# Moving loads and small stores between the stages of a backward kernel: gradient rows for a tail, zero columns of tap arrays, narrow rows

## The chip, the cores and the metric

The kernel runs on one core of one Trainium2 chip. The metric is the device time of one launch in microseconds. A profile is one execution taken by the hardware profiler; its span is a little shorter than the device time. The engines are named as in the profile: PE is TensorE (PEld its weight loads), DVE is VectorE, ACT is ScalarE, POOL is GpSimd, SP is SyncE. SP computes nothing here: it issues nearly all transfers, and SPq and ACTq in a view are the issues of SP and of ACT.

## The reference

The reference is one block of a speech model for two sequences of 4000 tokens with 144 channels, run forward and backward. It returns the output and the gradients of all eight inputs.

```python
xa = layernorm(x)
q, k, v = split(xa @ w_qkv)
glob = softmax(q @ k.T * D ** -0.5) @ v @ w_att_out          # global branch: attention
h = gelu(layernorm(x) @ w_mlp_in);  u, g = split(h)
gc = conv5(layernorm(g), dw_csgu)                            # 5 taps along the tokens
loc = (u * gc) @ w_mlp_out                                   # local branch
m = concat(glob, loc)
out = x + (m + conv5(m, dw_merge)) @ w_merge
_out, vjp = jax.vjp(forward, x, w_qkv, ..., w_merge)
return (_out, *vjp(grad_out))
```

## The kernel before

**Stages.** For each of the two sequences (index b) the kernel runs three stages: a head, attention with the local branch inside it, and a tail. A token block has 128 tokens, so a sequence has 32 blocks; a group g is four blocks, so there are 8 groups. The 144 channels don't fit 128 partitions: the first 128 go one way, and the last 16 ("narrow rows") another.

**Head** (`phase_head`). `take_go` fetches the rows of `grad_out` for one group into a tile `gs`, five shifted copies for the five taps, 720 KB, through `go_taps` (lines 1095 to 1118; group 0 takes four transfers, because the rows before the first token are zeros that POOL writes at L1106). `narrow` gathers the last 16 channels of the five copies into a tile `g80` on POOL (L1436). `stA` transposes both on PE (L1473 and L1478); ACT and DVE copy them out (L1474, L1481, the latter into `go80`). `stT` transposes the normalised input (L1486, L1490). `stB` makes Q and the gradients that enter the two branches (PE L1506 to L1515, copies on ACT L1508, L1518 and DVE L1516). In the first sequence the head also prepares weights, among them `W.c80` in `Weights.rest` (L1360, L1361). At n == 5 `spread` sends the narrow rows of the normalised input, sixteen partitions of `R`, to DRAM (L1525, tensor `R_d`) and into the arrays that attention reads (L1529).

**Attention** (`phase_attn`) runs over 32 rows of blocks and is written out by hand: `unit` makes scores and their gradients (L1975, L1979, then ACT L1987 and DVE L1989), `flip` transposes them by DMA (L1997), `yz` (L2025) and `xfill` (L2047, L2048) use them two rows later. Between these the class `Steps` places the local branch, `local_steps`, a pair of blocks at a time. A pair starts with a matmul on the wide rows and one on the narrow rows (L1803, L1804); the narrow ones lie in a tile `Rz`, 128 partitions that are zero but for the last sixteen, loaded from `R_d` (`load_R`, L1783). The convolutions of the local branch pass through four DRAM arrays (`Taps`), whose columns before the first token and after the last must be zero; the constructor writes them with two small transfers each (L1625, L1626).

**Tail** (`phase_tail`): each of its 8 groups needs a `gs` again. Groups 0, 3 and 6 take it from a pool `S.early` that exists from the start of the kernel, the others from a pool of the tail. The first tail also normalises the second sequence's input and fetches the first three `gs` tiles for its head (L2350, steps NPR - 1 to NPR + 1 of the tail, NPR = 16). At its end it copies a partial sum out (`grs`, ACT L2282) and sends it to DRAM (`gr_d`, L2283).

**What sets the order.** Every engine runs its own list in order; a wait at the head of a list holds all that is behind it. SP's list holds nearly all transfers. In the built program of before the four transfers of a tail's group 0 stand far ahead of that tail: for the first sequence among the first loads of the first head, for the second at the end of the first tail, among the loads of the second head.

Of the kernel before, what the change touches and what calls it, by code (L numbers as in the profile page):

```python
# [7 lines left out]
BF = mybir.dt.bfloat16  # L8
# [6 lines left out]
D = 144  # L15
# [1043 lines left out]
NBK = 32  # L1059
# [61 lines left out]
class Weights:  # L1121
# [3 lines left out]
    def __init__(self, k, W, tmp):  # L1125
        self.k, self.W, self.tmp = k, W, tmp
# [163 lines left out]
    def rest(self, pst, ps):  # L1290
# [67 lines left out]
        pt = ps.tile([128, 512], F32, tag="w", name="fw")  # L1358
        for v in range(2):
            nc.tensor.matmul(pt[0:80, v * DR:(v + 1) * DR], self.e5[v][0:5].rearrange("p a b -> p (a b)"), self.cw[0:5, 2 * D + 128:3 * D], start=True, stop=True)  # L1360
            nc.vector.tensor_tensor(W.c80[0:80, v, :], pt[0:80, v * DR:(v + 1) * DR], self.i80[0:80, :], op=ALU.mult)  # L1361
        for h in range(2):
            A = self.A[h]
# [75 lines left out]
def take_go(k, S, b, g, ld):  # L1439
    gs = S.gs[g] = ld.tile([128, 4, 5, D], BF, tag="gs", name="gs")  # L1440
    go_taps(k, gs, b, g, k.nc.sync)


def phase_head(k, W, b, S, nrm, ld, wts):

    nc, tc = k.nc, k.tc
    with ExitStack() as es:
# [13 lines left out]
        id_ = W.ident  # L1461
        S.QB = S.ab.tile([128, 4, 128], BF, name="QB")
        nc.vector.memset(S.QB[:], 0.0)

        def narrow(g):
            if g not in S.g80:
                narrow_go(k, S, g, ld)
# [55 lines left out]

        def spread():
            nc.sync.dma_start(S.R_d[:], R[112:128, :])  # L1525
            for q in range(2):
                for r in (2 * q, 2 * q + 1):
                    for c0, c1, x in S.XRw:
                        nc.sync.dma_start(x[32 * r:32 * r + DR, :, 0:SC], R[112:128, 0:TT_].rearrange("p (a h c) -> p a h c", h=2, c=SC)[:, c0:c1, q, :])  # L1529
# [16 lines left out]
        with tc.manual_schedule():  # L1546
            rest = None
            for g in range(3):
                if g not in S.gs:
                    take_go(k, S, b, g, ld)  # L1550
            if wts:
                wts.heads(ps_t, ps_2, lambda: nrm.stats(0))
                nrm.power(0)
                wts.taps1(0)
                wts.keys(ps_t, ps_2)
                nrm.shift(0)
                nrm.apply(0)
                narrow(0)
                wts.taps()
                wts.taps1(1)  # L1560
                nrm.stats(1)
                nrm.power(1)
                stA(0)
                take_go(k, S, b, 3, ld)
                stT(0)
                wts.rows(ps_2, 0)
                nrm.shift(1)
                nrm.apply(1)
                narrow(1)
                nrm.stats(2)  # L1570
                nrm.power(2)
                wts.rows(ps_2, 1)
                rest = wts.rest(ps_t, ps_2)
            else:
                narrow(0)
                narrow(1)
                stA(0)
                take_go(k, S, b, 3, ld)
                stT(0)
            for n in range(-1, NGR):  # L1580
                if 1 <= n + 2 < NGR:
                    stT(n + 2)
                if n == 3:
                    jit0()
                if n >= 0:
                    stB(n, *tiles())
                if 1 <= n + 2 < NGR:
                    stA(n + 2)
                if wts and n + 3 < NGR:
                    nrm.shift(n + 3)  # L1590
                    nrm.apply(n + 3)
                if n + 3 < NGR:
                    narrow(n + 3)
                if wts and n + 4 < NGR:
                    nrm.stats(n + 4)
                    nrm.power(n + 4)
                if n + 5 < NGR and n + 5 not in S.gs:
                    take_go(k, S, b, n + 5, ld)
                for f in put_dug[:len(put_dug) - n % 2]:
                    f()  # L1600
                del put_dug[:len(put_dug) - n % 2]
                if n == 5:
                    spread()
                if n == 4:
                    jit()
                if rest:
                    next(rest, None)
            for _ in rest or ():
                pass
            for f in put_dug:  # L1610
                f()
            del put_dug[:]
# [3 lines left out]
class Taps:  # L1616
# [1 line left out]

    L = 2 + NBK * 128 + 2

    def __init__(self, k, name, zero):
        self.nc = k.nc
        self.a = k.tc.dram_tile([80, self.L], BF, name=name)
        with self.nc.allow_non_contiguous_dma(reason="two columns before the first"):
            self.nc.sync.dma_start(self.a[:, 2:4], zero[0:80, 0:2])  # L1625
            self.nc.sync.dma_start(self.a[:, self.L - 4:self.L - 2], zero[0:80, 0:2])  # L1626
# [14 lines left out]
class Chan:  # L1641

    def __init__(self, k, W, pool, ps, name, zero):
        self.k, self.W, self.pool, self.ps, self.name = k, W, pool, ps, name
        self.t, self.r, self.kept, self.kept8 = {}, {}, {}, {}
        self.taps = Taps(k, name + "_d", zero)

    def put(self, p, src):  # L1650
        nc = self.k.nc
# [112 lines left out]
def local_steps(k, W, b, S, es, ps, Q):  # L1764
# [4 lines left out]
    on = es.enter_context(tc.tile_pool(name="lo_on", bufs=1, reuse_waits="tile"))  # L1769
    zero = on.tile([128, 2], BF, name="lo_zero")  # L1770
    nc.gpsimd.memset(zero[:], 0.0)
    gnC = Chan(k, W, wk, ps, "gnC%d" % b, zero)
    dgC = Chan(k, W, wk, ps, "dgC%d" % b, zero)
    S.taps = [Taps(k, n + "80_%d" % b, zero) for n in ("y", "u")]
    dws = on.tile([128, NBK // 2, 5], F32, name="dws")
    dw8 = on.tile([128, NBK // 2], F32, name="dw8")
    jg = on.tile([128, 256], BF, name="jg")
    Rz = [on.tile([128, 256], BF, name="Rz%d" % n) for n in range(2)]
    for t in Rz:
        nc.gpsimd.memset(t[:], 0.0)  # L1780

    def load_R(p):
        nc.sync.dma_start(Rz[p % 2][112:128, :], S.R_d[:, p * 256:(p + 1) * 256])  # L1783
    load_R(0)
    id_ = W.ident
    NPR = NBK // 2

    def pair(p):
# [2 lines left out]
            return tuple(((n, p - d), 0) for n, d in keys if p >= d)  # L1791
        yield 'P', 0, aft(("z", 1), ("h", 2))
        R = Rz[p % 2]
        if p + 1 < NPR:
            load_R(p + 1)
        hs = wk.tile([128, 2, 2 * D], BF, tag="hs", name="hs")
        sq = wk.tile([128, 2, 2 * D], BF, tag="sq", bufs=1, name="sq")
# [16 lines left out]
        nc.vector.tensor_tensor(a_[:], a_[:], hs[:], op=ALU.mult)  # L1814
        Q.mark("z", p)
        yield 'V', 2
        nc.scalar.activation(a_[:], a_[:], ACT.Tanh)
        yield 'V', 2, aft(("ug", 4)), .8
        h_ = wk.tile([128, 2, 2 * D], BF, tag="h_t", bufs=4, name="h_t")
# [106 lines left out]
def phase_attn(k, W, b, S):  # L1926
# [3 lines left out]
    with ExitStack() as es:  # L1930
# [137 lines left out]
        with tc.manual_schedule():  # L2068
            local_steps(k, W, b, S, es, ps_f, Q)
            for g in range(1, NGR):  # L2070
                Q.add(32 * g - 16, jit(g))
            left = list(range(NGR, 2 * NGR))
            for i in range(NBK + 2):
                if i == NBK:
                    Q.rate = Q.most = 1.8
                pr, half = i // 2 - 1, i % 2
                for c2 in range(4):
                    if 4 * i + c2 <= 4 * NBK:
                        unit(4 * i + c2)
                    for place in range(2):  # L2080
                        if place == 0 and 0 <= i - 2 < NBK:
                            yz(i - 2, c2)
                        if (i, c2, place) in ((0, 0, 0), (0, 1, 0), (0, 2, 0), (0, 3, 0), (0, 3, 1), (1, 0, 0), (1, 1, 0), (1, 1, 1)):
                            S.stB(left.pop(0), lambda: ps_y.tile([128, 2, D], F32, tag="y", name="pq"), lambda: ps_x.tile([128, 2 * D], F32, tag="x", name="pb"),
                                  lambda: xp.tile([128, 4, D], BF, tag="xs", name="dug"))
                            if not left:
                                nc.vector.memset(P[:, 2, TT_:], 0.0)
                        for f, rows in fills.get((half * 4 + c2, place), ()):
                            if 0 <= pr < NBK // 2:
                                xfill(pr, f, rows)  # L2090
                        Q.place()
                        for key, fi, h in {(0, 0): (("PT", i - 1, 1),), (1, 0): (("ST", i - 1, 1),), (2, 1): (("PT", i, 0),), (3, 1): (("ST", i, 0),)}.get((c2, place), ()):
                            if 0 <= fi < NBK:
                                flip(key, fi, h)
            while Q.tasks:
                Q.place()


def phase_tail(k, W, b, S, nrm, nxt):
# [3 lines left out]
    with ExitStack() as es:  # L2103
# [20 lines left out]
        def loads(g):  # L2124
            r = slice(g * 4, g * 4 + 4)

            one = g % 3 == 0
            gs = S.early.tile([128, 4, 5, D], BF, tag="gs", name="gs") if one else ld.tile([128, 4, 5, D], BF, tag="gs", name="gs")
            go_taps(k, gs, b, g, nc.sync)
            ug = S.early.tile([128, 4, D], BF, tag="ug", name="ug") if one else ld.tile([128, 4, D], BF, tag="ug", name="ug")  # L2130
            nc.sync.dma_start(ug[:], S.ug_d[:, r, :])
            G["ug", g], G["gs", g] = ug, gs
# [153 lines left out]
        with tc.manual_schedule():  # L2286
# [6 lines left out]
            for h in range(NPR + 5):  # L2293
# [52 lines left out]
                    dx_mm(h)  # L2346
                if hf == 0 and 0 <= g - 1 < NGR:
                    load_x(g - 1)
                if nrm and NPR - 1 <= h < NPR + 2:
                    take_go(k, nxt, 1, h - NPR + 1, nrm.ld)  # L2350
                if hf == 1 and g + 2 < NGR:
                    load_dh(g + 2)
                    loads(g + 2)
# [346 lines left out]
```

## Time and profile before

| | |
|---|---|
| device time, median of 3 runs | 1292.65 us (1290.83 to 1294.41) |
| span of the profiled execution | 1286.6 us |
| PE busy | 1210.9 us, 94% |
| DVE / ACT / POOL busy | 960.4 / 843.3 / 559.4 us |
| moved by DMA | 205.44 MB, mean 160 GB/s |

In the first sequence the head lies at 0 to 51 us, attention at 51 to 553 us and the tail from there; the second head begins at 641 us, its attention at 670 us and the last tail at 1175 us. Busy shares are means over these stages. What the edits touch is the few microseconds at the joints between stages, so the joints are read one by one.

### The profile page before, as it was taken

Reading aid. Unit: us, or ns where it says so; the run is one execution under the profiler, and the core shown is the slowest. Engines: PE = TensorE matmul, PEld = TensorE weight load, DVE = VectorE, ACT = ScalarE, POOL = GpSimd, SP = SyncE. Lnnn points to the kernel's source line nnn. Section 1 sums busy time; section 2 is a strip of 40 time slices with the busy share of each in tenths; the row PEclk is TensorE's granted clock in tenths of the full one; section 3 lists DMA queues with packets and bytes.
Section 4 is the critical chain, followed back from the end, with each engine's and each line's share of the span. In section 5 each row is a group of like instructions: output and inputs, shape, how many; then the busy total and the mean of one; then the engine's idle time right before and its main releaser. Section 6 shows DMA issues by size and latency. Waiting matters only on the chain.

```text
span 1286.6 us, 39804 instructions
## 1 busy us (share of the span) xinstructions
PE 1210.9 (94%) x15118; PEld 949.2 (74%) x15118; DVE 960.4 (75%) x3257; ACT 843.3 (66%) x2494; POOL 559.4 (43%) x1011
## 2 busy tenths in 40 slices
PE   7799999999999999989988999999999999998995
PEld 4567777777777777789964777777777777778984
DVE  7467788888788887857535677888888878885774
ACT  5677777777777766556555777776776777654542
POOL 7213444444445432356511244454544445334650
PEclk9999999999999999999988999999999999999998
DMA  7379999998898999968755798899998998998861
GB/s 232 79 144 168 144 166 157 154 160 159 157 161 150 159 166 158 161 191 220 205 168 102 142 165 149 152 164 162 160 165 150 159 166 155 162 160 179 240 165 30
DMA packets 633617, 205.44 MB, mean 160 GB/s; under 512 B 576719, under 2 KB 630948, under 8 KB 633380
## 3 DMA queue, kind: packets, MB, share of 16 engines
q1 hardware_dynamic: 626912, 197.46, 81.7%
q10 hardware_dynamic: 6500, 5.32, 1.7%
q8 instruction: 120, 1.97, 0.6%
q14 instruction: 85, 0.70, 0.2%
HBM read 46.14 MB, written 21.79 MB: 53 GB/s over the span
## 4 chain that ended last, share of the span: by engine, by line
PE 66%; DVE 14%; DMA 6%; issue 5%; ACT 4%; SPq 2%; POOL 2%; ACTq 0%; DVEq 0%; POOLq 0%
PE y L2025 15%; PE pS L1979 9%; PE X L2047 8%; PE X L2048 8%; PE pD L1979 7%; PE pS L1975 5%; DVE Sm L1989 5%; PE pc L1684 2%; PE pb L1514 2%; DMA gs<-in_grad_out_dram 2%; DVE jg L1906 2%; DMA u<-r 1%; DVE acc L2063 1%; ACT Qs L2008 1%; PE pD L1975 1%
## 5 line engine op out<-in xcount | busy, mean ns | idle before, releaser
L1989 DVE SCALAR_TENSOR_TENSOR Sm<-pD,Pm 128x500 bf16<-128x500 f32 x512 | 325.7, 673 | 92.5 <-PE pD L1979 58.6
L1987 ACT ACTIVATE Pm<-pS 128x500 bf16<-128x500 f32 x512 | 295.9, 586 | 41.4 <-PE pS L1979 38.6
L2047 PE MATMUL X<-Qs,Sm 128*128 128x144 bf16 x2048 | 285.6, 226 | 9.5 <-DVE acc L2063 9.1
L2060 POOL TENSOR_TENSOR acc<-xs,acc 128x432 f32<-128x432 f32 x150 | 169.2, 1128 | 279.8 <-ACT xs L2059 279.4
L2048 PE MATMUL X<-Bt,Pm 128*128 128x144 bf16 x2048 | 285.4, 226 | 0.6 <-DVE Bt L2012 0.6
L2048 PEld LDWEIGHTS <-Pm 128*128 128x128 bf16 x2048 | 200.2, 98 | 12.1 <-issue 11.5
L2047 PEld LDWEIGHTS <-Sm 128*128 128x128 bf16 x2048 | 200.1, 98 | 1.5 <-issue 0.9
L2025 PEld LDWEIGHTS <-PT 128*128 128x128 bf16 x2048 | 136.6, 98 | 30.7 <-issue 2.8
L2025 PEld LDWEIGHTS <-ST 128*128 128x128 bf16 x2048 | 136.4, 98 | 27.6
L2059 ACT COPY xs<-X 128x432 f32<-128x432 f32 x150 | 78.0, 520 | 111.3 <-PE X L2048 102.1
L2063 DVE TENSOR_TENSOR acc<-X,acc 128x432 f32<-128x432 f32 x180 | 104.0, 578 | 53.2 <-PE X L2048 52.7
L1987 ACT ACTIVATION_READ_ACCUMULATOR Pm<-pS 128x1 f32 x512 | 104.8, 205 | 0.0
L1975 PE MATMUL pD<-rb,QBr 16*128 16x500 bf16 x448 | 95.7, 379 | 3.5 <-DVE Sm L1989 3.0
L1979 PEld LDWEIGHTS <-BTm 128*128 128x128 bf16 x512 | 49.9, 98 | 60.0 <-issue 2.0
L1975 PE MATMUL pS<-rb,QBr 16*128 16x500 bf16 x448 | 92.1, 380 | 0.5 <-DMA rb<-Sm 0.2
L1906 DVE SCALAR_TENSOR_TENSOR jg<-gnC,dgC 128x256 bf16<-128x256 bf16 x160 | 88.9, 556 | 1.0
L1979 PEld LDWEIGHTS <-QTm 128*128 128x128 bf16 x512 | 29.0, 97 | 73.2 <-issue 73.2
L2035 POOL TENSOR_TENSOR B_t<-zd,yd 128x144 bf16<-128x144 f32 x64 | 34.0, 531 | 112.2 <-ACT zd L2034 111.8
L1979 PE MATMUL pS<-ra,QTm 128*128 128x500 bf16 x256 | 76.9, 382 | 0.0
L1979 PE MATMUL pS<-rb,QTm 128*128 128x500 bf16 x256 | 76.6, 381 | 0.0
L2025 PE MATMUL y<-ra,PT 128*128 128x144 bf16 x1024 | 74.3, 226 | 1.3 <-ACT zd L2034 1.3
L2025 PE MATMUL y<-rb,PT 128*128 128x144 bf16 x1024 | 74.3, 226 | 1.1 <-ACT zd L2034 1.1
(638 smaller groups left out, 2885.1 us busy)
## 6 DMA issues: line engine op xcount, KB each, us to landing
gs<-in_grad_out_dram SPq DMA_DIRECT2D x24, 720.0 KB
dh_d<-dh SPq DMA_DIRECT2D x32, 144.0 KB
dhr<-dh_d SPq DMA_DIRECT2D x16, 288.0 KB
gs<-in_grad_out_dram SPq DMA_DIRECT2D x8, 540.0 KB
xg<-in_x_dram SPq DMA_DIRECT2D x21, 144.0 KB
dug_d<-dug SPq DMA_DIRECT2D x16, 144.0 KB
dug<-dug_d SPq DMA_DIRECT2D x32, 72.0 KB
ug_d<-ug SPq DMA_DIRECT2D x32, 72.0 KB
```

What stands on the lines that cost most here:

```text
L1906: nc.vector.scalar_tensor_tensor(jg[:], a_[:, m:m + 256], 1.0, d_[:, 2:258], op0=ALU.mult, op1=ALU.mult, accum_out=dws[:, p, m:m + 1])
L1975: nc.tensor.matmul(o_[h][:, 0:SC], jt[i // 4][2][rr, i % 4, :], S.XR[c2][rr, 0:SC], start=True, stop=False)
L1979: nc.tensor.matmul(o_[h][:, 0:SC], jt[i // 4][w][:, i % 4, :], S.xaT[:, c0:c0 + SC], start=False, stop=True)
L1987: nc.scalar.activation(P[:, pb, c1:c1 + SC], o_[h][:, 0:SC], ACT.Exp, accum_out=ld8[:, 0, n_:n_ + 1])
L1989: nc.vector.scalar_tensor_tensor(Sm[:, pb, c1:c1 + SC], o_[h][:, 0:SC], 1.0, P[:, pb, c1:c1 + SC], op0=ALU.mult, op1=ALU.mult, accum_out=l ...
L2025: nc.tensor.matmul(y[:, w, :], src[:, jj, :], S.xaa[:, j, :], start=(j == 0), stop=(j == NBK - 1))
L2035: nc.gpsimd.tensor_tensor(S.Zn[:, i, :], zd[:], yd[:], op=ALU.add)
L2047: nc.tensor.matmul(X[:, jj, :], Sm[:, i % NP, j * 128:(j + 1) * 128], Qs[:, i % 4, :], start=(kk == 0 and jj == 0), stop=False, skip_group ...
L2048: nc.tensor.matmul(X[:, jj, :], P[:, i % NP, j * 128:(j + 1) * 128], Bt[:, i % 4, :], start=False, stop=(kk == 1), skip_group_check=True)
L2059: nc.scalar.copy(xs[:, 0:nj, :], X[:, 0:nj, :])
L2060: nc.gpsimd.tensor_tensor(a_, xs[:, 0:nj, :], a_, op=ALU.add)
L2063: nc.vector.tensor_tensor(a_, X[:, 0:nj, :], a_, op=ALU.add)
```

## The change

It moves transfers and a few instructions; the arithmetic is the same.

1. **Tail rows.** The `gs` of a tail's group 0 is fetched near the end of attention (row 32, column step 1), behind the last transposes, and no longer in a head. In the first tail the three `gs` loads for the next head start one step earlier.
2. **Zero columns.** The zero columns of the four tap arrays are sent from the first two pairs of the local steps, between other work, not all at once when the local steps are set up.
3. **Narrow rows.** The `Rz` tiles live in the head's pool and get their first two contents directly from `R` in on-chip memory, beside the other sends of `spread`; only pairs from 2 on read `R_d`.
4. **Two small orders in the first head.** The two matmuls of `c80` are issued before the two multiplications that read their bank; `narrow(0)` comes ahead of `apply(0)` on POOL.

```diff
@@ Weights.rest
         for v in range(2):
             nc.tensor.matmul(pt[0:80, v * DR:(v + 1) * DR], self.e5[v][0:5].rearrange("p a b -> p (a b)"), self.cw[0:5, 2 * D + 128:3 * D], start=True, stop=True)
+        for v in range(2):
             nc.vector.tensor_tensor(W.c80[0:80, v, :], pt[0:80, v * DR:(v + 1) * DR], self.i80[0:80, :], op=ALU.mult)
@@ phase_head
         nc.vector.memset(S.QB[:], 0.0)
+        S.Rz = [S.ab.tile([128, 256], BF, name="Rz%d" % n) for n in range(2)]
+        for t in S.Rz:
+            nc.gpsimd.memset(t[:], 0.0)
...
         def spread():
             nc.sync.dma_start(S.R_d[:], R[112:128, :])
+            for p in range(2):
+                nc.sync.dma_start(S.Rz[p][112:128, :], R[112:128, p * 256:(p + 1) * 256])
...
                 nrm.shift(0)
+                narrow(0)
                 nrm.apply(0)
-                narrow(0)
@@ Taps
-    def __init__(self, k, name, zero):
+    def __init__(self, k, name):
         self.nc = k.nc
         self.a = k.tc.dram_tile([80, self.L], BF, name=name)
+
+    def clear(self, zero):
         with self.nc.allow_non_contiguous_dma(reason="two columns before the first"):
             self.nc.sync.dma_start(self.a[:, 2:4], zero[0:80, 0:2])
             self.nc.sync.dma_start(self.a[:, self.L - 4:self.L - 2], zero[0:80, 0:2])
@@ local_steps
-    Rz = [on.tile([128, 256], BF, name="Rz%d" % n) for n in range(2)]
-    for t in Rz:
-        nc.gpsimd.memset(t[:], 0.0)
+    Rz = S.Rz
...
-    load_R(0)
...
-        if p + 1 < NPR:
+        if 2 <= p + 1 < NPR:
             load_R(p + 1)
...
         Q.mark("z", p)
         yield 'V', 2
+        for t in ([gnC.taps, dgC.taps], S.taps, [], [])[min(p, 3)]:
+            t.clear(zero)
         nc.scalar.activation(a_[:], a_[:], ACT.Tanh)
@@ phase_attn
                             yz(i - 2, c2)
+                        if (i, c2, place) == (NBK, 1, 1):
+                            S.gs0 = S.early.tile([128, 4, 5, D], BF, tag="gs", name="gs")
+                            go_taps(k, S.gs0, b, 0, nc.sync)
@@ phase_tail
-            gs = S.early.tile([128, 4, 5, D], BF, tag="gs", name="gs") if one else ld.tile([128, 4, 5, D], BF, tag="gs", name="gs")
-            go_taps(k, gs, b, g, nc.sync)
+            if g == 0:
+                gs = S.gs0
+            else:
+                gs = (S.early if one else ld).tile([128, 4, 5, D], BF, tag="gs", name="gs")
+                go_taps(k, gs, b, g, nc.sync)
...
-                if nrm and NPR - 1 <= h < NPR + 2:
-                    take_go(k, nxt, 1, h - NPR + 1, nrm.ld)
+                if nrm and NPR - 2 <= h < NPR + 1:
+                    take_go(k, nxt, 1, h - NPR + 2, nrm.ld)
```

More of the change, by code (lines that the diff above doesn't have):

```diff
@@ L1641, with __init__ @@
 class Chan:
-    def __init__(self, k, W, pool, ps, name, zero):
+    def __init__(self, k, W, pool, ps, name):
         self.k, self.W, self.pool, self.ps, self.name = k, W, pool, ps, name
         self.t, self.r, self.kept, self.kept8 = {}, {}, {}, {}
-        self.taps = Taps(k, name + "_d", zero)
+        self.taps = Taps(k, name + "_d")
     def put(self, p, src):
@@ L1771, in local_steps @@
     nc.gpsimd.memset(zero[:], 0.0)
-    gnC = Chan(k, W, wk, ps, "gnC%d" % b, zero)
-    dgC = Chan(k, W, wk, ps, "dgC%d" % b, zero)
-    S.taps = [Taps(k, n + "80_%d" % b, zero) for n in ("y", "u")]
+    gnC = Chan(k, W, wk, ps, "gnC%d" % b)
+    dgC = Chan(k, W, wk, ps, "dgC%d" % b)
+    S.taps = [Taps(k, n + "80_%d" % b) for n in ("y", "u")]
     dws = on.tile([128, NBK // 2, 5], F32, name="dws")
```

## The prediction

> **What bounds the kernel now.** I read the busy shares first (PE 94%), then who waited for whom in the long stage, then PE's timeline at each joint. In the list of PE's waits from 85 to 540 us, most of the first attention, the largest entries are
>
> ```profile
> PE X L2047 <- DVE acc L2063: 4.6, 6, 1.7
> PE pD L1975 <- DVE Sm L1989: 2.1, 9, 0.4
> ```
>
> (total, times, longest). All of that list comes to some 10 us in 455, so PE bounds attention: what PE gains ahead of it stays gained. PE's timeline shows where it stands still at the joints:
>
> ```profile
> 38.87 0.16 PE L1360 MATMUL fw<-w_cw,w_e 5*80 5x16 bf16 x1 [2.99 <-DVE w_c L1361]
> 57.06 0.28 PE L1804 MATMUL ph<-w_i,Rz 128*128 128x288 bf16 x1 [3.12 <-DMA Rz<-R_d]
> 647.16 0.58 PE L1473 MATMUL tp<-w_ident,gs 128*128 128x128 bf16 x4 [4.24 <-DVE go80f L1481]
> 679.48 0.40 PE L1804 MATMUL ph<-w_i,Rz 128*128 128x288 bf16 x1 [5.83 <-DMA Rz<-R_d]
> ```
>
> The bracket is the idle time and what ended it: 16.2 us in four waits. The last three cost more than they show. In the table by stretches (length, then busy time of PE, PEld, DVE, ACT, POOL, then the granted PE clock, DMA share and GB/s) the clock is halved after each:
>
> ```profile
> 58.00:60.00 2.00, 2.00 (x10) 1.13 (x9) 1.13 (x3) 1.57 (x6) 0.00 (x0) 0.50 0.00 0
> 648.00:650.00 2.00, 2.00 (x17) 1.75 (x16) 0.85 (x2) 1.36 (x3) 0.46 (x1) 0.50 0.63 178
> 680.00:682.00 2.00, 2.00 (x9) 0.60 (x6) 0.11 (x1) 1.65 (x5) 0.00 (x0) 0.50 0.00 0
> ```
>
> After the wait at 38.87 it is not: that stretch is at 1.00. The waits at 57.06 and 679.48 lie behind this stretch of SP's issues (start, length), which on the chain of waits stands in one line from the last send of the head to `Rz`:
>
> ```profile
> 54.89 0.43 SPq L1626 DMA_DIRECT2D u<-lo_zero  x1
> 55.44 0.81 SPq L1783 DMA_DIRECT2D Rz<-R_d  x2
> ...
> 676.92 0.42 SPq L1626 DMA_DIRECT2D u<-lo_zero  x1
> 677.46 0.82 SPq L1783 DMA_DIRECT2D Rz<-R_d  x2
> ```
>
> Eight zero stores (51.64 to 55.32, and 672.68 to 677.34) go ahead of a load that lands 1.5 to 1.9 us after its issue. The wait at 647.16 goes back to DVE, and from there to a transfer:
>
> ```profile
> 646.69 0.42 DVE L1481 COPY go80f<-tp 80x512 bf16<-80x512 bf16 x1 [4.82 <-DMA gr_d<-grs]
> ```
>
> `go80f` lies where the tail kept `grs`, so it waits until `gr_d` has been read out: issued at 641.39, landed at 646.57. Ahead of it SP issued, from 625.6 to 640.75, four gradient groups of about 720 KB, one of them for the tail 500 us later; the DMA engines are at 0.97 to 1.10 from 642 to 648 us.
>
> **What the Trainium skill says.** "TensorE: Matmul & The Clock Gate", section "What's actually happening": the clock falls to half after an idle window of about 3.4 us and comes back after about as long a busy one, the window running free. The trace agrees: 3.12, 4.24 and 5.83 us of idleness halved it, 2.99 did not. "DMA: Bandwidth & Descriptors", section "Anatomy of one DMA": about 2 us of fixed cost for a transfer, whatever its size (stated for another issue path); `Rz<-R_d`, 8 KB, takes 1.5 and 1.9 here. "SBUF — State Buffer", section "Terms": DVE and GpSimd share a port pair, and the loser blocks fully. At 9.26 two `apply` instructions on POOL take 2.43 us where later ones take 0.92, beside DVE's L1244 (9.08 to 10.79), so I expect `narrow(0)` to change little there.
>
> **The change part by part.**
>
> *Narrow rows, first joint.* `Rz` is sent right behind `R_d` (46.2 us), so it lands near 48.5, five microseconds ahead of its use at 53.9. The 3.12 us go. So does the half clock: PE was busy through 58 to 62 us at 0.50 and 0.67, a loss of 1.0 + 0.7 = 1.7. ACT, next in line, was idle 2.90 us in the same wait and keeps up later (2.94 us busy in 4 at 62 to 66). Sum 4.8. Second joint: 5.83, and 2.52 us busy at 0.50 (678 to 682) and 2.0 at 0.86: 1.3 + 0.3. Against it the two sends push the last eight sends of `spread` back by 2 x 0.43 us, and there PE's L1975 already waits 0.22 us for one at 670.90: minus 0.9. In the first joint the same send landed before PE wanted it, so nothing. Sum 6.5.
>
> *Zero columns.* Sixteen transfers of 0.42 us of SP are not saved, only moved. The first four of a sequence go behind the last `dug_d` store (about 79 us), the other four between transposes of rows 1 and 2 (about 94). What is queued behind each four, 1.8 us, is a `flip` that PE uses more than a row of blocks (some 14 us) later. Price 0. `gnC_d` gets its first store after them in the same list.
>
> *Tail rows out of the joint at 641.* Two things change ahead of `gr_d`: 717 KB less, and the next head's groups 0 to 2 issued one step earlier, with the third just before `gr_d`. By SP's list I put them at about 623.5, 632 and 634. At the 190 GB/s of 625 to 641 and up to 300 in the stretches around it, they are through by 639 to 640. `grs` is ready at 640.2 (ACT 639.50 + 0.70), which PE sets; `gr_d` can go at 640.3 and, 288 KB in an empty queue, land at 642.5 to 643.5 (estimate from the 3.78 us of 720 KB at 571.74). PE runs dry at 642.9. So 3.6 to 4.2 of the 4.24 us go, and with them the half clock: 0.84 us at 0.50, 2.0 at 0.50, 2.0 at 0.54, together 2.3. Groups 3 to 7 are fetched when a tile comes free, so earlier too; each has over 2.6 us, one PE step of that head (653.33 to 655.95), and I keep 0.5 for a late one. Sum 6.0. The input rows of the tail's last group now go behind group 0 and hold DVE's `stats` (626.99) by up to 2 us; PE's two output tiles cover that, as the DVE copies behind it (629.28, 631.54) are wanted only at 632.4 and 635.9. One POOL memset of 0.69 us moves to idle time.
>
> *Tail rows into the end of attention.* The four transfers go at the end of the last transposes' issues, 546.8 and 1168.1 us. DMA is nearly idle then:
>
> ```profile
> 550.00:552.00 2.00, 2.00 (x36) 2.00 (x34) 1.32 (x6) 0.44 (x3) 0.72 (x1) 1.00 0.03 8
> 552.00:554.00 2.00, 2.00 (x36) 2.00 (x34) 0.46 (x1) 0.95 (x3) 1.27 (x2) 1.00 0.22 31
> ```
>
> (1172 to 1174 likewise: 0.01.) The rows are wanted at 553.8 and 1175.1, 7.0 us after the first issue. Nearest rows: a 720 KB group took 3.78 us at 571.74 and 7.31 at 1177.79, in company. From both ends that is landed 2 us early or about 2 us late, twice; in a hole I take on time, and 0.5 for each tail: minus 1. The `dh_d` stores behind them leave 1.9 us later; the `dhr` load behind those waits for PE until 552.57 anyway.
>
> *First head.* `c80`: PE's second L1360 no longer waits for the L1361 that stands behind DVE's stats and five L1356. PE goes on to L1486, which needs ACT's second L1429 (to 37.25), and two pb's that have free banks; the third would want the bank that DVE frees at 38.9. L1473 then starts at 39.5 where it started at 41.15: 1.6 (ends: 0.5, 2.9). With group 0 landing earlier than 9.74 and `g` no longer last, PE's L1478 at 12.29 leaves the path: 0.4.
>
> Sum: 4.8 + 6.5 + 6.0 + 1.6 + 0.4 - 1.0 = 18.3 us; 1292.65 - 18.3 = 1274.4.
>
> **The rivals.** *The waits move, half stays.* Another wait takes the place: the sends of `spread` late by 0.9 at both joints, gradient groups late in the second head by 3, both tails late by 2 each, the clock still halved at 647 (2.3 not gained): 18.3 + 1.0 - 0.9 - 2.5 - 4 - 2.3 = 9.6, so 1283. For it: the DMA engines are at 0.6 to 1.1 in that head, and group 3 held POOL at 651.9. Against: PE never stood there but once. *More is freed.* DMA traffic in the heads (1.12 to 1.24 from 8 to 14 us) slows more than I see, and no tail waits: 18.3 + 1 + 3 = 22.3, 1270. *The late fetch hurts.* The transposes of the last row and the tail's first loads share the queue; if 717 KB ahead of them are exposed whole (7.3 us, twice) and the zero stores too (16 x 0.45 = 7.2), that is 21.8 lost for 18.3 + 1 gained, 1295, slower. Against: the last transposes are issued before, and PE waits for no transpose in the list above.
>
> **How the numbers follow.** Forecast 0.66, half 0.20, more 0.09, slower 0.03, and 0.02 for a sum of nothing. The range runs from 1269 to 1284: down past the freer case, up to the half one. Faster 0.95, same 0.02, slower 0.03.
>
> **What would show it.** Right: no `Rz` wait on PE, both joints at clock 1.00; L1481 at the second head's start within a microsecond of PE's last L2202; L1360 without a wait; EF L2177 at a tail's start with no DMA wait. Wrong: a wait of PE's L1975 on the `spread` sends over 1 us, of L1473 on `gs` in the second head, of L2177 or POOL's L2139 on `gs` in a tail's first microseconds, or of L2025 on a transpose about 100 us.

## The result, and the profile after

| | median us | runs | lowest to highest | span of the profiled run |
|---|---|---|---|---|
| before | 1291.74 | 4 | 1288.57 to 1294.41 | 1286.6 |
| after | 1279.10 | 4 | 1277.05 to 1280.23 | 1278.3 |

The ratio is 0.9901 with a 95% interval of 0.9874 to 0.9929. On 1291 us that is 12.8 us less (9.2 to 16.3); the forecast was 18.3 less. Of the prediction's own figures the rival "the waits move, half stays" (9.6 less) lies nearer to this than the forecast does. The two profiles differ by only 8.3, because the profiled run of after was the slowest of its four and that of before the fastest.

PE's timeline of the kernel after, at the places of the four long waits of before (start, length, and in brackets the idle time with what ended it):

```profile
38.80 0.68 PE L1490 MATMUL pm<-w_ident,ra 128*128 128x128 bf16 x4 [0.99 <-ACT ra L1430]
51.18 0.37 PE L1982 MATMUL pS<-rb,QBr 16*128 16x500 bf16 x1 [0.21 <-DMA rb<-Sm]
52.81 0.37 PE L1982 MATMUL pS<-rb,QBr 16*128 16x500 bf16 x1 [1.26 <-DMA rb<-Sm]
...
645.90 1.38 PE L1518 MATMUL pb<-w_GL,Pm 128*128 128x288 bf16 x5 [2.66 <-POOL Pm L1456]
...
670.35 0.37 PE L1982 MATMUL pS<-rb,QBr 16*128 16x500 bf16 x1 [1.35 <-DMA rb<-Sm]
```

All four waits of before are gone, and at each place a shorter one stands: 16.2 us became 6.5. Both `Rz` waits became waits for `rb`, the rows of R that the scores need, which leave in the same list of sends just behind `Rz` (in the views R goes by the name of its tile, `Sm`). The wait for `go80f` became one for a GpSimd memset, a few instructions further on. Next the clock, in the table by stretches (length; busy time of PE, PEld, DVE, ACT, POOL; granted PE clock; DMA share; GB/s):

```profile
20.00:22.00 2.00, 1.33 (x11) 1.12 (x12) 1.71 (x10) 0.58 (x1) 1.66 (x3) 0.65 0.77 285
22.00:24.00 2.00, 2.00 (x10) 1.28 (x9) 0.31 (x1) 0.60 (x2) 0.00 (x0) 0.50 0.00 0
58.00:60.00 2.00, 2.00 (x16) 1.00 (x14) 0.66 (x4) 1.38 (x6) 0.00 (x0) 1.00 0.07 23
...
646.00:648.00 2.00, 2.00 (x9) 1.25 (x10) 0.31 (x1) 0.09 (x1) 0.92 (x3) 0.50 0.22 76
648.00:650.00 2.00, 2.00 (x17) 1.69 (x15) 0.45 (x2) 0.84 (x3) 0.00 (x0) 0.50 0.00 0
650.00:652.00 2.00, 2.00 (x16) 1.65 (x14) 0.71 (x2) 1.10 (x3) 0.00 (x0) 0.50 0.73 245
680.00:682.00 2.00, 2.00 (x18) 1.43 (x17) 1.35 (x5) 1.66 (x6) 0.00 (x0) 1.00 1.06 199
```

Both joints (58, 680) run at full clock now. The second head (646 to 652) is still halved, and a stretch at 20 to 24 is halved that was at 1.00 before.

Why the memset is late shows in GpSimd's timeline:

```profile
644.96 0.46 POOL L1437 TENSOR_SCALAR g<-gs 128x320 bf16<-128x320 bf16 x1 [6.33 <-DMA gs<-in_grad_out_dram]
645.36 0.26 POOL L2627 MEMSET Pm<- 128x192 bf16 x1
645.55 0.26 POOL L2627 MEMSET Sm<- 128x192 bf16 x1
645.75 0.10 POOL L1456 MEMSET Pm<- 128x2 bf16 x1
645.78 0.18 POOL L1457 MEMSET Pm<- 128x98 bf16 x1
```

The two columns of zeros ahead of `goT` (L1456) take 0.10 us. They stand behind `narrow(3)`, which waits 6.33 us for the gradient rows of group 3. SP could issue these only at 640.22, because their tile came free with PE's first transposes of this very head (L1477, from 639.8). In the kernel before, the same memset was hidden under the wait for `go80f` (done at 647.1):

```profile
646.00 0.10 POOL L1455 MEMSET Pm<- 128x2 bf16 x1
```

The third new thing lies at the end of the first tail, on DVE and on PE:

```profile
625.68 0.31 DVE L1405 BATCH_NORM_STATS2 st<-xg 128x6 f32<-128x144 bf16 x1 [1.96 <-DMA xg<-in_x_dram]
...
628.37 0.24 PE L2216 MATMUL po<-w_G,r 80*128 80x144 bf16 x1 [1.51 <-DMA r<-u]
```

`r` is a small fetch (80 KB) that PE needs for the output product; before, no wait for it stood here. Why it comes late is read further down, beside a kernel without that wait.

Cut at the same instructions in both profiles, the gain falls as follows (times are first or last starts of a group):

| stretch, before | length before | after | gain | forecast |
|---|---|---|---|---|
| first head: start to first `pS` | 50.78 | 51.18 | -0.4 | 2.0 |
| first joint: `pS` to first `y` (84.9; 81.6) | 34.1 | 30.4 | 3.7 | 4.8 |
| first attention: to first tail's `EF` (553.8; 550.5) | 468.9 | 468.9 | 0.0 | -0.5 |
| first tail: `EF` to last `gr` (639.2; 638.1) | 85.4 | 87.6 | -2.2 | 0 |
| second head: to `pS` (670.30; 668.63) | 31.1 | 30.5 | 0.6 | 6.0 |
| second joint: to first `y` (707.1; 699.1) | 36.8 | 30.5 | 6.3 | 6.5 |
| the rest, to the end | 579.5 | 579.2 | 0.3 | -0.5 |

So the joints gave nearly what was forecast, and the tail rows, in two stretches (first tail and second head), nothing: -2.2 + 0.6. Of the 2.2 us, 1.5 are the wait for `r<-u`; PE's waits for POOL's `g` are 1.1 us longer too (3.9 and 5.0), but they lie between 3.2 and 5.0 in the fourteen kernels of this case and follow none of the edits. One profile of each kernel is thin evidence, so the parts were timed.

### The profile page after: what moved, and what is told of

Same layout as the page of the kernel before. It is cut to its first block, busy times and chain, and to the rows that moved or that the text cites. A ratio compares the mean times of both kernels' runs of the same rounds, so it can differ in the third digit from the quotient of the medians.

```text
span 1278.3 us, 39805 instructions
## 1 busy us (share of the span) xinstructions
PE 1210.3 (95%) x15118; PEld 949.6 (74%) x15118; DVE 959.7 (75%) x3257; ACT 842.4 (66%) x2494; POOL 556.2 (44%) x1011
## 3 DMA queue, kind: packets, MB, share of 16 engines
q1 hardware_dynamic: 626912, 197.46, 81.6%
## 4 chain that ended last, share of the span: by engine, by line
PE 66%; DVE 14%; DMA 7%; ACT 5%; issue 4%; POOL 2%; SPq 1%; ACTq 0%; DVEq 0%; POOLq 0%
PE y L2032 15%; PE pS L1986 9%; PE X L2054 8%; PE X L2055 8%; PE pD L1986 7%; PE pS L1982 5%; DVE Sm L1996 5%; PE pc L1692 2%; PE pb L1518 2%; DVE jg L1913 2%; DMA gs<-in_grad_out_dram 1%; PE gr L2286 1%; DMA y<-r 1%; DMA f_EF<-EF_d 1%; DVE acc L2070 1%
## 5 line engine op out<-in xcount | busy, mean ns | idle before, releaser
L2055 PEld LDWEIGHTS <-Pm 128*128 128x128 bf16 x2048 | 200.2, 98 | 11.9 <-issue 11.3
L1913 DVE SCALAR_TENSOR_TENSOR jg<-gnC,dgC 128x256 bf16<-128x256 bf16 x160 | 91.7, 573 | 1.0
```

The lines of the kernel that those rows point to most:

```text
L1913: nc.vector.scalar_tensor_tensor(jg[:], a_[:, m:m + 256], 1.0, d_[:, 2:258], op0=ALU.mult, op1=ALU.mult, accum_out=dws[:, p, m:m + 1])
L2055: nc.tensor.matmul(X[:, jj, :], P[:, i % NP, j * 128:(j + 1) * 128], Bt[:, i % 4, :], start=False, stop=(kk == 1), skip_group_check=True)
```

## The experiments

All are compared with the kernel before in runs of the same chip, by ratio; "us" is the ratio on 1291.

**The four parts alone**, each added to the kernel before. The diffs are those parts of the change (`Rz` in `spread` and out of `load_R`; `gs0` and `take_go`; `c80` and `narrow(0)`; `clear`).

| added alone | ratio | 95% interval | us |
|---|---|---|---|
| narrow rows straight (a_rz) | 0.9932 | 0.9912 to 0.9953 | -8.8 |
| zero columns (a_zero) | 0.9915 | 0.9895 to 0.9935 | -11.0 |
| first head (a_head) | 0.9982 | 0.9971 to 0.9994 | -2.3 |
| tail rows (a_tail) | 1.0005 | 0.9989 to 1.0022 | +0.6 |

Expected of narrow rows: 

> Before plus the straight loads of Rz alone (two sends of R in the spread, memsets in the head, no load through R_d for the first two pairs). Theory T1 (the forecast's sum was right part by part, and waits that the change adds took some of it back): the Rz waits of 3.1 and 5.8 us and their half clock go, and PE comes to wait for the XR rows (rb<-Sm) instead, some 1.3 us at each joint, so 11.3 - 2.6 + 0.9 (already counted) = about 9 us, 1282 to 1284. Theory T2 (the parts are worth what was forecast, and the loss is in the first head's clock and start): 11.3 us, near 1280.5. Theory T3 (freed waits move elsewhere and little stays): under 6 us, above 1286.

Expected of zero columns: 

> Before plus the zero columns alone: the eight zero stores leave SP's queue ahead of the two Rz loads and go out within the first three local steps. The Rz loads go 3.7 us earlier at the first joint and 4.7 us at the second, so although R_d is still on the way: T1, the R_d write lands before that, and most of the Rz waits goes without the straight loads: 7 to 10 us, 1282 to 1285. T2, the write of R_d, which the loads need, is what they wait for (R_d was sent by SP ahead of the XR rows, which take until then), and the gain is under 3 us.

Expected of the first head: 

> Before plus the first head's two edits alone (both c80 matmuls ahead of the two multiplies, narrow(0) ahead of the normalised rows of group 0). T1: the wait of 2.99 us at c80 goes and 1.5 to 2 us stay, 1290. T2: the head's other chain (ACT's ra) takes its place and nothing stays or it is slower, 1292 to 1293.5.

Expected of the tail rows: 

> Before plus the tail rows alone (gs of the tail's first group fetched at the end of attention, the three groups of rows of the next head one step earlier). T1: the wait of 4.24 us for go80f goes, but a wait for POOL's memset of goT's zero columns (2.7 us) with a half clock takes its place, and the rows sent one step earlier hold r<-u back (1.5 us) in the first tail: net about 1 to 2 us, 1289.5 to 1291. T2: 6 to 7 us as forecast, 1285.

The zero columns, which the prediction priced at 0, are worth as much alone as the straight loads. PE's waits from 615 to 690 us with the straight loads alone (total, times, longest):

```profile
PE tp L1476 <- DVE go80f L1484: 4.3, 1, 4.3
PE pS L1977 <- DMA rb<-Sm: 1.3, 1, 1.3
PE pq L1509 <- ACT Q_t L1511: 0.8, 1, 0.8
```

and with the zero columns alone:

```profile
PE tp L1473 <- DVE go80f L1481: 4.3, 1, 4.3
PE EF L2181 <- POOL g L2143: 1.1, 1, 1.1
PE ph L1806 <- DMA Rz<-R_d: 1.0, 1, 1.0
```

Either edit takes the `Rz` wait of 5.8 us away. The first leaves 1.3 us for `rb`, because two sends were put ahead of it. The second leaves 1.0 for `Rz`, still fetched through `R_d`: what had made it late was the queue ahead of the load, not the way through DRAM. Their sum would be 19.8 us, more than the whole change, so they are two ways to the same time. With the tail rows alone, in the same window:

```profile
PE ph L1804 <- DMA Rz<-R_d: 5.1, 1, 5.1
PE pb L1514 <- POOL Pm L1455: 2.7, 1, 2.7
PE po L2209 <- DMA r<-u: 1.8, 1, 1.8
```

`go80f` is gone, and the memset and `r<-u` have come, 4.5 us for 4.2. That is the tail edits' whole account, with nothing else changed: T1's waits are there, and T2's gain of 6 to 7 us is outside the interval. For the first head too T1 holds. For the zero columns T2 (under 3 us) is excluded, and T1's 7 to 10 us reach into the interval (8.4 to 13.6) from below. For the straight loads the time alone (8.8, within 6.1 to 11.4) doesn't tell 9 from 11.3, but the wait for `rb` that T1 names is there; under 6 us is just excluded.

**Two parts taken away from the changed kernel.** n_tail undoes both tail edits (first diff), n_rz the straight loads (second):

```diff
-                        if (i, c2, place) == (NBK, 1, 1):
-                            S.gs0 = S.early.tile([128, 4, 5, D], BF, tag="gs", name="gs")
-                            go_taps(k, S.gs0, b, 0, nc.sync)
...
-                if nrm and NPR - 2 <= h < NPR + 1:
-                    take_go(k, nxt, 1, h - NPR + 2, nrm.ld)
+                if nrm and NPR - 1 <= h < NPR + 2:
+                    take_go(k, nxt, 1, h - NPR + 1, nrm.ld)
```

```diff
...
-            for p in range(2):
-                nc.sync.dma_start(S.Rz[p][112:128, :], R[112:128, p * 256:(p + 1) * 256])
...
+    load_R(0)
...
-        if 2 <= p + 1 < NPR:
+        if p + 1 < NPR:
```

> The changed kernel without both of its edits to rows of a tail (gs of the tail's first group fetched in the head again, the next head's rows at the old steps). T1: the two edits together are worth nothing, as they were alone (ratio 1.0005 to before), so this stands at the changed kernel's time: 1277 to 1281, ratio 0.989 to 0.992. Rival: the tail edits are worth something only once the joints are mended: 4 us or more slower, above 1283.

> The changed kernel without the straight loads of Rz (R_d and load_R(0) and (1) as before), zero columns sent within the local steps. T1: with the zero stores gone from the queue the loads through R_d are nearly in time (alone they left 1.0 us at the second joint and nothing at the first), and XR rows leave SP 1.3 to 1.5 us earlier, so this is within 1.5 us of the changed kernel: 1277 to 1280. Rival: the straight loads carry the gain: 5 us or more slower.

Without the tail edits: 0.9917 (0.9900 to 0.9934), 10.7 us less than before. Without the straight loads: 0.9902 (0.9882 to 0.9921), as good as the whole change. In its profile `Rz<-R_d` costs PE 0.5 us at the second joint and `rb<-Sm` nothing. So the changed kernel is as fast without its straight loads, within the intervals, and the rival (5 us slower) is excluded. Whether it would be as fast without its zero columns instead wasn't run. The tail edits in their place are worth some 2 us, within the intervals of nothing, where 5.0 was forecast; their rival, 4 us slower than the change, is not quite excluded: it would be a ratio of 0.9932, inside the interval by a hair.

**Mends of the changed kernel.** m_memset puts the two memsets on VectorE in the second head, where they stand ahead of the first `go80f` copy; m_xrfirst moves the sends of XR ahead of `R_d` and `Rz`; m_tgundo sends the next head's rows at the old steps; m_all is the first two together, m_all_tg all three.

```diff
-        nc.gpsimd.memset(goT[:, 0:2], 0.0)
-        nc.gpsimd.memset(goT[:, 2 + TT_:], 0.0)
+        (nc.vector if b else nc.gpsimd).memset(goT[:, 0:2], 0.0)
+        (nc.vector if b else nc.gpsimd).memset(goT[:, 2 + TT_:], 0.0)
...
         def spread():
-            nc.sync.dma_start(S.R_d[:], R[112:128, :])
-            for p in range(2):
-                nc.sync.dma_start(S.Rz[p][112:128, :], R[112:128, p * 256:(p + 1) * 256])
             for q in range(2):
...
+            nc.sync.dma_start(S.R_d[:], R[112:128, :])
+            for p in range(2):
+                nc.sync.dma_start(S.Rz[p][112:128, :], R[112:128, p * 256:(p + 1) * 256])
```

> The changed kernel, with the two memsets of goT's zero columns in the second head on VectorE instead of GpSimd (behind narrow(3) there). T1: what the tail rows gained was taken back by the wait of 2.66 us for this memset and by the half clock that followed it (0.50 in 646 to 650, 0.74 to 654: some 2.5 us); both go, so 4 to 5 us off the changed kernel's 1279: 1274 to 1275. Rival: PE then waits for the next thing that hangs on the rows sent at 640.22 (narrow(3), for stA(3)) and under 1.5 us stay: above 1277.5.

> The changed kernel with the spread's sends of the XR rows (rb, ra <- Sm) ahead of R_d and the two straight sends of Rz. T1: the waits for rb<-Sm (1.26 + 0.21 us at the first joint, 1.35 at the second) go, since these sends leave 1.6 and 1.9 us earlier, and Rz, sent 3.5 to 5 us later, still lands ahead of its first reader at the first joint (needed near 54.5) and about on time at the second: 2 to 3 us off, 1276 to 1277. Rival: Rz becomes late at the second joint (eight sends of 0.6 us ahead of it) and takes back 1 to 3 us: 1278 to 1280.

> The changed kernel with the three groups of rows for the next head sent at the old step of the tail (h = NPR - 1 and on), all else as changed. T1: the wait of 1.51 us for r<-u and the 2.0 us hold of VectorE for xg in the first tail go (gr's series back from 14.1 to 12.3 us), but the wait for go80f of some 4 us at the second head's start comes back in place of the 2.66 us for the memset; so it stands within 2 us of the changed kernel: 1278 to 1281. Rival (the earlier rows are worth what was forecast): 4 us or more slower, above 1283.

> Both together: XR rows ahead of R_d and Rz, and the second head's memsets of goT on VectorE. T1: the two are at different places and add: 6 to 7.5 us off the changed kernel, 1271.5 to 1273. Rival: one of them buys nothing: 1274 to 1277.

> XR rows ahead of R_d and Rz, goT's memsets on VectorE in the second head, and the next head's rows at the old steps of the tail. T1 (the earlier rows cost more in the tail, 1.5 to 2.2 us for r<-u, a half clock and the hold of VectorE, than the 2.7 us wait for go80f that they save): a little below the 1272.2 of the kernel with the first two alone: 1269 to 1272. Rival (once the memset is out of the way, the earlier rows are worth their wait): 1274 to 1276.

| kernel | ratio to before | 95% interval | median us |
|---|---|---|---|
| the change | 0.9901 | 0.9874 to 0.9929 | 1279.10 |
| m_memset | 0.9892 | 0.9877 to 0.9906 | 1276.77 |
| m_xrfirst | 0.9909 | 0.9886 to 0.9931 | 1278.71 |
| m_tgundo | 0.9890 | 0.9875 to 0.9904 | 1275.85 |
| m_all | 0.9858 | 0.9842 to 0.9874 | 1272.23 |
| m_all_tg | 0.9873 | 0.9855 to 0.9892 | 1273.35 |

The three single mends can't be told from the change by time. m_memset and m_xrfirst were expected to give more than they measured, and the 4 to 5 us expected of m_memset lie outside its interval; the rival for m_tgundo, over 1283, is excluded, so the earlier rows are not worth 4 us. m_xrfirst (1272.43 to 1282.70) is too scattered to judge. The traces are clearer. The waits of PE in m_all from 605 to 690 us, all that are left:

```profile
PE po L2216 <- DMA r<-u: 2.2, 1, 2.2
PE pq L1510 <- ACT Q_t L1512: 0.8, 1, 0.8
PE po L2215 <- DVE og L2220: 0.6, 1, 0.6
PE po L2216 <- DMA r<-y: 0.6, 1, 0.6
PE pD L1982 <- DVE Sm L1996: 0.2, 1, 0.2
```

No wait for `Pm`, `rb` or `Rz`: each mend does away with its wait and calls up no new one at its place. But the wait for `r<-u` in the first tail is longer than the change's 1.5 us (2.2 here, 1.9 in m_memset), and in these two profiles the half clock stands behind it, at 626 to 632 and at 628 to 634, where the change ran at full clock. So in m_memset's profile a part of what the second head gained was lost again in the tail. Together the two mends stand 18.3 us below the kernel before (16.3 to 20.4), the figure of the forecast, but by other parts. That is the lowest median of all versions, and its interval only touches that of the change. How this splits between the two is open.

What the earlier rows do in the first tail shows when the stretches of the changed kernel

```profile
622.00:624.00 2.00, 1.51 (x24) 1.50 (x24) 1.65 (x8) 2.00 (x7) 1.98 (x4) 1.00 0.99 351
624.00:626.00 2.00, 2.00 (x35) 2.00 (x33) 0.31 (x1) 1.33 (x6) 0.79 (x1) 1.00 1.08 344
626.00:628.00 2.00, 0.86 (x14) 0.68 (x11) 1.87 (x11) 1.33 (x4) 0.39 (x1) 1.00 0.97 263
```

are put beside those of m_tgundo, where the same work runs about two microseconds earlier:

```profile
620.00:622.00 2.00, 1.63 (x26) 1.63 (x26) 1.93 (x7) 2.00 (x7) 1.92 (x4) 1.00 0.54 130
622.00:624.00 2.00, 2.00 (x35) 2.00 (x33) 1.86 (x11) 1.97 (x9) 0.78 (x3) 1.00 0.69 276
624.00:626.00 2.00, 2.00 (x35) 2.00 (x33) 0.75 (x4) 0.47 (x2) 1.92 (x4) 1.00 1.00 238
```

With the rows out one step earlier the DMA engines are at 0.97 to 1.08 just when `r<-u` (issued at 624.46) and `xg` have to come through; PE is busy 4.37 of these 6 us. With the rows at the old step the DMA share is 0.54 to 0.69 as they pass, PE is busy 5.63 of 6, and neither wait is there.

A full DMA is not all of it. In the changed kernel SP and ACT issued, in order of time:

```profile
620.65 0.53 SPq L1107 DMA_DIRECT2D gs<-in_grad_out_dram  x1
...
621.87 0.32 ACTq L1646 DMA_DIRECT2D r<-y  x1
...
624.46 0.32 ACTq L1646 DMA_DIRECT2D r<-u  x1
624.88 0.32 ACT L2242 ACTIVATE jka<-t 128x144 bf16<-128x144 f32 x1 [0.64 <-DMA gs<-in_grad_out_dram]
```

`r<-u` leaves 2.6 us behind its twin `r<-y`, and by the chain of waits its issue was held until the `gs` load of 620.65 had landed (624.38), though it takes nothing from it. Then it was 3.87 us on its way. All seven kernels with the earlier rows show this: in each the chain has a load of `gs` or `xg`, 2.7 to 4.3 us long, ahead of the issue of `r<-u`, and then 3.0 to 4.6 us to landing. In m_tgundo `r<-u` leaves 0.36 us behind `r<-y` (618.82); in the kernels without either tail edit it is about 2 us and costs PE 0.5 or less. What ties the two transfers isn't shown by the traces.

With the old step, in return, the wait for `go80f` is back:

```profile
640.68 0.58 PE L1477 MATMUL tp<-w_ident,gs 128*128 128x128 bf16 x4 [2.73 <-DVE go80f L1485]
```

It is 2.73 us, not 4.24, with the tail's own 717 KB still out of this head. The earlier step pays 1.5 to 2.2 us in the tail for 2.7 (2.1 in m_all_tg) in the head; a half clock followed in m_all's tail on the one side, and in the heads of m_tgundo and m_all_tg on the other. m_all against m_all_tg, 1.5 in a thousand apart with overlapping intervals, doesn't say which is better.

**The memset, tested without the rest.** b_tail_ms adds the tail rows and the moved memsets to the kernel before.

> The kernel before plus the two tail edits alone, and goT's memsets of the second head on VectorE. T1 (the tail rows' gain was taken by the memset's wait of 2.7 us and a half clock of 1.7 us): 4 us below the tail edits alone, 1286 to 1288, ratio 0.996 to 0.998. Rival (the wait merely moves on, to the second joint's Rz or to the next thing in the second head): the same as the tail edits alone, ratio 0.999 to 1.001.

It measured 0.9982 (0.9971 to 0.9994), 2.3 us less than before, where the tail rows alone stood at 1.0005 (0.9989 to 1.0022). The two intervals overlap by a hair (0.9989 to 0.9994), but the difference, 3.0 us, is just clear of zero: the half-widths of the two intervals, combined, come to 2.6. So by time moving the memset gave 0.4 to 5.6 us, with the 4 that T1 expects inside, and the rival (no difference) is excluded only narrowly. The profile says it more plainly; the waits of PE from 605 to 690 us, all that are left:

```profile
PE ph L1804 <- DMA Rz<-R_d: 5.0, 1, 5.0
PE po L2209 <- DMA r<-u: 2.3, 1, 2.3
PE po L2208 <- DVE og L2213: 0.6, 1, 0.6
PE pt L2159 <- ACT hT L2199: 0.3, 1, 0.3
```

The second head is without a wait of PE's and at full clock, and the second joint's `Rz` wait has not grown.

## Why the prediction was right or wrong

The sign and the joints were right; of 18.3 us, 12.8 came.

- **Second joint, 6.5.** Right: 6.3 in the profiles, with the full clock at 680. That the pushed sends cost about what was reckoned (1.1 forecast, 1.35 found) is luck: the two `Rz` sends took 1.53 us of SP, not 0.86, and the eight behind them were 0.7 us quicker than before (665.49 to 670.72; 665.59 to 671.49).
- **First joint, 4.8.** 3.7. The step that failed: "In the first joint the same send landed before PE wanted it, so nothing." The two `Rz` sends took 1.26 us together, the four sends of `rb` behind them 3.67, where before they had taken 2.69, and PE waited 0.21 + 1.26. Before, then after:

```profile
46.53 2.69 SPq L1529 DMA_DIRECT2D rb<-Sm  x4
...
46.65 1.26 SPq L1531 DMA_DIRECT2D Rz<-Sm  x2
47.95 3.67 SPq L1535 DMA_DIRECT2D rb<-Sm  x4
```

The last send was over at 51.62 instead of 49.22. The margin of before was never read off; it was smaller than this shift of 2.4 us.

- **Zero columns, 0.** Right only as the last of the two edits. It was listed as work "only moved"; alone it gives 11.0 us (8.4 to 13.6), because the eight stores were what the `Rz` load stood behind. The prediction's own reading, "eight zero stores go ahead of a load", said so, and the sum then gave all of it to the other edit.
- **Tail rows out of the joint, 6.0.** This is the term that failed. Its first half held: `gr_d` left at 639.05 (640.3 expected), `go80f` was written from 641.36 on, and the 4.24 us went. What failed is that PE would then run on. A few instructions later it needs a memset that GpSimd holds behind `narrow(3)`, and that hangs on the group of rows still issued in the head. Of groups 3 to 7 the prediction said "fetched when a tile comes free, so earlier too; each has over 2.6 us". Group 3 left 3.0 us earlier (640.22, not 643.19), but PE came to the memset 6.1 us earlier (643.24; the matmul behind it started at 649.30 before). The 0.5 us kept for such a late group became 2.66, and the half clock (2.3 in the sum) stayed, with 6 us at 0.50 and so 3.0 lost in the profile of after.
- **The stats, "PE's two output tiles cover that".** Right as far as it goes: DVE was held 1.96 us, as forecast, and PE's wait for DVE's `og` stayed at 0.6 us. But the sum left out `r<-u`, a fetch by ACT's queue that the earlier rows hold up: PE stopped for it for 1.51 us, and 1.1 to 2.3 in the six other kernels with the earlier rows; with the old steps it is 0.5 or less.
- **Tail rows into the end of attention, -1.0.** Nothing was lost: neither tail's first `EF` waits for a transfer.
- **First head, 2.0.** Alone 2.3 (0.8 to 3.7), right. In the profile of after it doesn't show, since PE started 0.7 us later (the wait for `w_l_s` is 2.09 us against 1.41) and the stretch at 20 to 24 ran at half clock. With `narrow(0)` moved up, PE's wait for `g` fell from 1.83 to 0.35 us there, and 0.48 came back as a wait for POOL's `ra`; the 0.4 us put down for it are too few to be told by time.
- **The rivals.** "The waits move" named three of the right places, the sends of `spread`, a gradient group in the second head and the clock at 647, but charged both tails for the late fetch, which cost nothing. "The late fetch hurts" and "more is freed" both fell: neither tail waited for it, and the time is not below the forecast.
- **"The trace agrees".** The waits that halved the clock were 3.12, 4.24 and 5.83 us long, but 3.12 us is already shorter than the idle window of about 3.4 us that was cited; the last section has more of this.

## What to carry to other kernels

When a wait is taken away, follow the engine to the next instructions behind it and ask what each of them hangs on: here a memset of 0.10 us, harmless for as long as it was hidden, made PE wait 2.66 us, and its move gave about 3 us in the kernel with the tail rows alone, since it stood in an in-order queue behind an operation on late data. Put constants ahead of anything that waits for a transfer, or on an engine that waits for none. And where several edits shorten one wait, price each alone and all together: two edits that each clear the same queue are worth one. And a small fetch that an engine needs soon should not be issued behind a bulk load that nobody needs yet: here `r<-u`, 80 KB, was held up by loads for the next head.

## What was not expected of the hardware

The same wait halves the clock in one run and not in another. PE's wait for `c80` is alike in the kernels with the old head; in that of zero columns alone it reads

```profile
40.42 0.17 PE L1360 MATMUL fw<-w_cw,w_e 5*80 5x16 bf16 x1 [2.99 <-DVE w_c L1361]
```

and its stretches after it

```profile
42.00:44.00 2.00, 2.00 (x11) 1.19 (x9) 0.32 (x2) 0.54 (x2) 0.00 (x0) 0.50 0.74 258
44.00:46.00 2.00, 2.00 (x17) 1.72 (x16) 0.50 (x2) 0.84 (x3) 0.00 (x0) 0.50 0.00 0
```

are at 0.50, where before, after the same 2.99 us, they were at 1.00. Of five profiles with this wait, two (a_zero, a_tail) were halved. Likewise the wait of 2.6 to 2.7 us for `Pm` halved the clock in the changed kernel, a_tail and m_xrfirst, but not in n_rz. So "2.99 did not halve it" was one draw, and no threshold. Shorter waits went ahead of a half clock too: in n_tail 1.25 us for `rb` at 51.42, and then 0.65 and 0.50 in the stretches from 52 to 56. The Trainium skill, "TensorE: Matmul & The Clock Gate", section "What's actually happening", says that the window runs free and that the clock falls after an idle window of about 3.4 us. A window that runs free would fit the two outcomes of one wait; but waits of 3.12, 2.66 and 1.25 us are shorter than that window, and the clock was halved after them all the same, so the measurement decides.

How long a half clock lasts can be read off the stretches: in the profile of after, 0.65 in 20 to 22 is 1.4 us at half, and with the 2.0 of 22 to 24 that makes 3.4 us, which costs 1.7 us of work; in the second head it is about 0.8 + 6.0, twice as long. The profiles of kernels that share a wait differ by one or two such pieces; whether they also make up the scatter between runs of one kernel isn't shown. The stretch at 20 to 24 was halved in six of the nine kernels with the new head and in none of the five with the old one; what sets it off wasn't settled.
